# Reciprocals and accumulator adds on GpSimd, P^T written over P, and a new order: two concatenated attention blocks on one core

## The chip, the core and the metric

One core of a Trainium2 chip runs the whole program. The metric is the time of one execution on the device in microseconds (us); the median of the runs shown stands for a kernel. The engines are named as the profile names them: PE (TensorE), PEld (its weight loads), DVE (VectorE), ACT (ScalarE), POOL (GpSimd) and SP (SyncE, which here only issues transfers).

## The reference

Two attention blocks with one set of shapes, A with 4 key/value heads for 32 query heads and B with 32 of each. Their results are concatenated along the last axis.

```python
# B=16 sequences, Sq=32 query tokens, D=1024, 32 query heads, Sk=1024 keys, Dh=128; all bf16
def block(x, k_cache, v_cache, wq, wo):          # A: 4 kv heads, each repeated 8 times; B: 32 kv heads
    q = (x @ wq) split into 32 heads
    scores = einsum("bhqd,bhkd->bhqk", q, k) * Dh ** -0.5
    p = softmax(scores, axis=-1)
    o = einsum("bhqk,bhkd->bhqd", p, v)
    return merge_heads(o) @ wo
out = concatenate([block(A...), block(B...)], axis=-1)
```

## The kernel before

**Work units.** The attention is cut into quads of 128 rows: 128 of block A (four query heads that share one K and V) and 128 of block B (two heads of two sequences, four different K and V). One quad goes through a fixed line of steps: scores on PE into two PSUM banks (L1003 for A, L1032 for B, where two quads are made together from 32x32 pieces of the array); the negated row maximum on DVE (L1044); exp on ACT, which writes P in bf16 and the row sum into `stat` (L1057); four PE transposes of P, taken as pairs of bf16 in f32 (L1069); the copy of P^T out of PSUM (`PT_ev`, through the helper `evac`, L643); P^T times V (L1089 for A, L1102 for B); the reciprocal of the row sum on DVE (`st_recip`, L1110); the multiplication by it (`norm`, L1118 on ACT, L1119 on DVE); a PE transpose of the result (L1125) and its copy into `OTA_sb` or `OTB_sb`.

**Around the quads.** K of block B is transposed in place by DVE in 32x32 pieces (L984), K of block A by PE (L977). Query projections (L734, L753) feed later quads. When a group of quads is done, the output projection `oproj` (L823) makes 512-wide results in one PSUM bank each: the first block of heads of an output is copied into `acc` (f32, SBUF), 64 later results are added to it by DVE (L835), and the last ones are added with a bf16 result (L844, and L839 for the last row group), which is sent out: by POOL's queue (L847, seven times) and at the very end by SP's (L841).

**What sets the order.** `list_schedule` builds the whole program as a list before it is emitted. It knows a duration for each step (`DUR`), the transfers' times, the buffers of each kind (`SLOTS`: 8 PSUM banks, 4 buffers for P, 4 for P^T, 8 for `stat`, 6 for O), and where PE must read another 16 KB piece of its program (`FETCH_BLOCK`, `FETCH_US`, `pe_pos`). It picks the next instruction by ranks; `TUNE` names one of 16 rank rules for each stretch of 40 choices. Copies and `norm` may go to ACT or DVE (`evac` with no engine). Each engine then executes its own list in order and waits on semaphores for what others make; a transfer is issued by SP once the buffer that it overwrites has been read.

**Late in the program** buffers that are done with are used again: K of B also goes to `wq_sb`, V of B to `xT_sb`, `QT_sb` and at last to `KB_sb`, and P of some quads to `xT_sb`.

Of the kernel before, what the change touches and what calls it, by code (L numbers as in the profile page):

```python
# [34 lines left out]
            "qprojA": 4, "qprojB": 4, "oprojA": 4, "oprojB": 4, "xT_tr": 16}  # L35
FETCH_BLOCK = 252
FETCH_US = 6.2
LOOK = 0.35
# [3 lines left out]
FREE_BANKS = 2  # L42
WINDOW = 40
RANKS = ((3.5, 122, 0.35, 0.0, 0.3), (3.0, 122, 0.35, 0.0, 0.3), (4.0, 122, 0.35, 0.0, 0.3), (3.5, 122, 0.15, 0.0, 0.3), (2.5, 122, 0.35, 0.0, 0.3), (5.0, 122, 0.35, 0.0, 0.3),
         (3.5, 122, 0.7, 0.0, 0.3), (3.5, 120, 0.35, 0.0, 0.3), (3.0, 124, 0.2, 0.0, 0.3), (3.5, 122, 0.15, 1.5, 0.3), (3.5, 122, 0.15, -1.5, 0.3), (3.5, 122, 0.15, 0.0, 0.0),
         (3.5, 122, 0.15, 0.0, 0.7), (3.5, 122, 0.15, 4.0, 0.3), (3.5, 122, 0.15, -4.0, 0.3), (3.5, 122, 0.25, 0.0, 0.3))
TUNE = (2, 5, 12, 2, 2, 2, 8, 9, 10, 10, 2, 0, 14, 11, 6, 10, 5, 14, 7, 0, 1, 9, 11, 15, 15, 8, 8, 15, 11, 3, 3, 8, 6, 3, 4, 14, 2, 5, 1, 10, 10, 14, 3, 2, 7,
        14, 14, 14, 14, 14, 14, 7, 12, 3, 11, 1, 9, 9, 9, 0, 7, 12, 4, 10, 9, 0, 10, 1, 14, 7, 0, 10, 10, 3, 10, 12, 8, 8, 14, 15, 12, 0, 7, 2, 15, 12, 4, 1,
        13, 7, 11, 13, 13, 10, 11, 7, 12, 8, 7, 14, 5, 15, 2, 9, 6, 12, 8, 1, 12, 12, 8, 13, 12, 14, 13, 11, 1, 12, 2, 9, 14, 12, 4, 14, 2, 14, 6)
HOLD_AHEAD = 1  # L50
# [15 lines left out]
    "o_fin@act": (0.47, 0.13),  # L66
    "KBt_tr": (1.15, 0.11), "max": (1.12, 0.11), "recip": (0.06, 0.11), "norm@dve": (0.265, 0.13), "PT_ev@dve": (0.58, 0.12),
    "OT_ev@dve": (0.13, 0.12), "KTA_ev@dve": (0.58, 0.12), "QBt_tr": (0.345, 0.10), "acc+": (0.58, 0.12), "accF": (0.59, 0.12),
    "qA_ev@dve": (0.58, 0.12), "qB_ev@dve": (0.58, 0.12), "xT_ev@dve": (0.60, 0.12), "o_fin@dve": (0.58, 0.12), "QR_ev@dve": (0.58, 0.12),
# [45 lines left out]

SLOTS = {"bank": 8, "P": 4, "PT": 4, "stat": 8, "O": 6}

# [11 lines left out]
class Prog:  # L129
# [120 lines left out]
    def list_schedule(self, lat=0.05, look=LOOK):  # L250
# [144 lines left out]

        pe_pos = [0]
        pe_have = {0: 0.0, 1: 0.0}
# [23 lines left out]
        while True:  # L421
            best = None
            bkey = None
            turn = len(order) // WINDOW
            turn = TUNE[turn] if turn < len(TUNE) else 0
# [128 lines left out]
def build(nc, pa, pb, out):  # L554
# [34 lines left out]
    with stack:  # L589
# [6 lines left out]
        ident = sb("ident", [P, P], BF)  # L596
        id32 = sb("id32", [P, P], F32)
        stat = sb("stat", [P, SLOTS["stat"], 4], F32)
        xT_sb = sb("xT_sb", [P, 2, DJ, NTOK], BF)
# [15 lines left out]
        P_sb = sb("P_sb", [P, SLOTS["P"], Sk], BF)  # L615
        PT_sb = sb("PT_sb", [P, SLOTS["PT"], NCH, P], BF)
        O_sb = sb("O_sb", [P, SLOTS["O"], Dh], BF)
# [12 lines left out]
        for idt, key in ((ident, "ident"), (id32, "id32")):  # L630
            pr.add("pool", lambda g, idt=idt: g.memset(idt[:], 0.0), writes=[key], name="c0")
            pr.add("pool", lambda g, idt=idt: g.affine_select(idt[:], idt[:], [[1, P]], ALU.not_equal, 1.0, base=0, channel_multiplier=-1),
                   writes=[key], name="c1")

        def evac(dst_ap, src_ap, reads, writes, name, eng=None, wtag=None, rtag=None, mul=None):
# [172 lines left out]
        def oproj(pi, blk, G):  # L808
# [7 lines left out]
            for oh in range(NOH):  # L816
# [15 lines left out]
                if blk == 0:  # L832
                    evac(a_ap, lambda v=v: bank(v)[:, 0:OUTW], reads=[], writes=[v, ("acc", pi, G, oh)], name="acc0")
                elif blk < nblk - 1:
                    pr.add("dve", lambda e, a_ap=a_ap, v=v: e.tensor_tensor(a_ap, a_ap, bank(v)[:, 0:OUTW], ALU.add),  # L835
                           reads=[], writes=[v, ("acc", pi, G, oh)], name="acc+")
                elif final:
                    o_ap = woA_sb[:, oh, 0:OUTW]
                    pr.add("dve", lambda e, a_ap=a_ap, o_ap=o_ap, v=v: e.tensor_tensor(o_ap, a_ap, bank(v)[:, 0:OUTW], ALU.add),  # L839
                           reads=[("acc", pi, G, oh)], writes=[v, ("woA", oh)], name="accF")  # L840
                    pr.add("sp", lambda e, o_ap=o_ap, oh=oh: e.dma_start(out_flat[G * P:(G + 1) * P, cols[pi] + oh * OUTW:cols[pi] + (oh + 1) * OUTW], o_ap),  # L841
                           reads=[("woA", oh)], dma_key=f"outf{oh}", name="outh_dma", dur=P * OUTW * 2)
                else:
                    pr.add("dve", lambda e, a_ap=a_ap, o_ap=o_ap, v=v: e.tensor_tensor(o_ap, a_ap, bank(v)[:, 0:OUTW], ALU.add),  # L844
                           reads=[], writes=[v] + [("acc", pi, G, x) for x in range(oh + 1)], name="accF")
# [70 lines left out]
        XK = 4 * LATE + 4 + NKB  # L916
        XV = 2 * LATE + 2 + 1

# [28 lines left out]
        def tile_v(t, x):  # L947
# [62 lines left out]

        def pt_of(v):
            return PT_sb[:, v.idx, :, :].rearrange("p c q -> p (c q)") if isinstance(v, Virt) else p_of(v)

        def st_scoresB(qs):
            n = qs[0].pn
            for q in qs:
                score_buf(q)
                q.vP, q.vPT = (("xT", 0, q.e), ("xT", 0, 2 + q.e)) if n >= XT_FREE and n % 2 else (Virt("P"), Virt("PT"))
                q.vO = Virt("O")
# [16 lines left out]
            kt = [(home_k(4 * q0.pn + x), ("T", 4 * q0.pn + x)) for x in range(4)]  # L1036
            halves = [("KV", r_[1]) for r_, _ in kt] if 2 * n == V_LAST - 4 else []
            for fp_ in range(4):
# [23 lines left out]
        def st_ptr(q):  # L1062
            vP, vPT, vb = q.vP, q.vPT, q.vbt

            def e_pt(e):
# [4 lines left out]
                return last  # L1070
            pr.add("pe", e_pt, reads=[vP, "id32", vPT], writes=[vb], name="PT_trA" if q.pi == 0 else "PT_trB")

        def st_pev(q, eng=None):
            vPT, vb = q.vPT, q.vbt
            evac(lambda: pt_of(vPT).bitcast(F32), lambda: bank(vb), reads=[], writes=[vb, vPT],
                 name="PT_ev", eng=eng)

        def ptc_of(vPT, c, lo, hi):
            return pt_of(vPT).rearrange("p (m r two) -> p m r two", m=NPK, two=2)[:, c // 2, lo:hi, c % 2]

        def st_pvA(q):
            vPT, vb = q.vPT, q.vbo
            gp = (q.s * NG + q.G) % 2
            kvs = q.kvslot

            def e_pv(e):
                last = None
                for c in range(NCH):
                    last = e.matmul(bank(vb)[:, 0:Dh], ptc_of(vPT, c, 0, P), VA_sb[:, kvs, c, :], start=(c == 0), stop=(c == NCH - 1))  # L1089
                return last  # L1090
            pr.add("pe", e_pv, reads=[vPT, ("VA", kvs)], writes=[vb], claims=[("OT", 0, gp, q.hh0 + a_) for a_ in range(4)], name="PVA",
                   rtag={("VA", kvs): q.kid})

        def st_pvB(q):
            vPT, vb = q.vPT, q.vbo
            gp = (q.m * NG + q.G) % 2

            def e_pv(e):
                last = None
                for c in range(NCH):  # L1100
                    for x in range(4):
                        last = e.matmul(bank(vb)[32 * x:32 * x + 32, 0:Dh], ptc_of(vPT, c, 32 * x, 32 * x + 32), tile_v(q.t, x)[:, c * Dh:(c + 1) * Dh],  # L1102
                                        start=(c == 0), stop=(c == NCH - 1), tile_position=(0, 32 * x))
                return last
            pr.add("pe", e_pv, reads=[vPT] + [res_v(q.t, x) for x in range(4)], writes=[vb], claims=[("OT", 1, gp, q.e + 2 * i) for i in range(2)],
                   name="PVB", tag="B%d" % q.t, rtag=dict((res_v(q.t, x), ("V", q.t, x)) for x in range(4)))

        def st_recip(q):
            vst = q.vst
            pr.add("dve", lambda e: e.reciprocal(stat[:, vst.idx, 2:3], stat[:, vst.idx, 1:2]), writes=[vst], name="recip")  # L1110

# [229 lines left out]
```

## Time and profile before

| | |
|---|---|
| median of 3 runs (lowest, highest) | 842.84 us (841.28, 844.58) |
| the profiled execution | 842.9 us, of which the span of its instructions 841.1 us |
| busy in the span | PE 747.0, DVE 718.6, ACT 609.9, POOL 5.0 us |
| TensorE clock granted, mean | 0.985 |
| moved by the 16 DMA engines | 341.68 MB, 406 GB/s over the span |

The busy times are sums over the span. A row of groups gives the line, engine, operation, output and input, count, then busy us and mean ns of one, then the idle time before them and what ended most of it. A row of stages gives the busy us of each engine, the granted clock, the DMA engines' busy share and the rate.

### The profile page before, as it was taken

The numbers are of one execution on the slowest core, as the hardware profiler recorded it, in microseconds if no ns is written. First come the engines' busy times: TensorE is split into PE (matmuls) and PEld (weight loads), VectorE is DVE, ScalarE is ACT, GpSimd is POOL, SyncE is SP. The second block draws the span as 40 slices with busy tenths as digits, with TensorE's granted clock in tenths as the row PEclk, the third lists the DMA queues.
The fourth block names the chain that finished last, engine by engine and source line by source line (L and its number), as shares of the span: only waits on it lengthen the run. The fifth ranks groups of instructions, "written<-read, shape, count | busy, mean of one in ns | idle before, by whom it ended". The sixth has DMA issues, their size and how long they took to land.

```text
span 841.1 us, 29570 instructions
## 1 busy us (share of the span) xinstructions
PE 747.0 (89%) x12864; PEld 475.3 (57%) x12864; DVE 718.6 (85%) x1016; ACT 609.9 (73%) x1361; POOL 5.0 (1%) x15
## 2 busy tenths in 40 slices
PE   5979899999989989999898999899988888878877
PEld 3456566666556556555565565555655546555654
DVE  0588888989889889898998898898989879989996
ACT  3378778878868667678778777677867758776773
POOL 0000000000000000000000000000000000000000
PEclk9999999999999999999999999999999999989999
DMA  9999999999999999999999999999999999999994
GB/s 340 420 415 419 412 410 418 416 416 415 419 413 416 416 419 411 413 393 417 419 404 416 418 414 421 418 397 418 417 417 406 415 416 420 416 384 403 417 416 198
DMA packets 56144, 341.68 MB, mean 406 GB/s; under 512 B 16144, under 2 KB 16400, under 8 KB 25040
## 3 DMA queue, kind: packets, MB, share of 16 engines
q1 hardware_dynamic: 55456, 337.97, 98.1%
q8 instruction: 101, 1.65, 0.8%
q0 software_dynamic: 560, 1.84, 0.5%
q14 instruction: 27, 0.22, 0.1%
HBM read 337.64 MB, written 2.10 MB: 404 GB/s over the span
## 4 chain that ended last, share of the span: by engine, by line
PE 50%; DVE 18%; ACT 14%; DMA 13%; issue 3%; SPq 2%; DVEq 0%; ACTq 0%
PE psum L1069 11%; ACT P_sb L1057 9%; DVE stat L1044 8%; DMA KB_sb<-in_B_k_cache_dram 8%; PE psum L823 8%; DVE KB_sb L984 7%; PE psum L1032 6%; PE psum L1102 6%; PE psum L734 5%; PE psum L1089 4%; PE psum L753 4%; PE psum L1003 3%; DMA VB_sb<-in_B_v_cache_dram 2%; PE psum L977 2%; PE psum L1125 1%
## 5 line engine op out<-in xcount | busy, mean ns | idle before, releaser
L1044 DVE TENSOR_REDUCE stat<-psum 128x1 f32<-128x1024 f32 x256 | 302.7, 1209 | 48.2 <-PE psum L1032 30.7
L1057 ACT ACTIVATE P_sb<-psum,stat 128x1024 bf16<-128x1024 f32 x246 | 274.9, 1119 | 60.6 <-DVE stat L1044 57.9
L984 DVE STREAM_TRANSPOSE KB_sb<-KB_sb 128x1024 f32<-128x1024 f32 x240 | 284.7, 1221 | 15.4 <-DMA KB_sb<-in_B_k_cache_dram 15.0
L1069 PE MATMUL psum<-id,P_sb 128*128 128x128 f32 x984 | 170.1, 303 | 19.3 <-ACT P_sb L1057 15.3
L1069 PEld LDWEIGHTS psum<-id,P_sb 128*128 128x128 f32 x984 | 139.8, 209 | 56.4 <-ACT P_sb L1057 40.4
L643 ACT COPY PT_sb<-psum 128x512 f32<-128x512 f32 x232 | 132.7, 598 | 26.5 <-PE psum L1069 23.9
L1118 ACT ACTIVATE O_sb<-psum,stat 128x128 bf16<-128x128 f32 x216 | 78.0, 376 | 47.5 <-PE psum L1089 20.3
L1003 PE MATMUL psum<-KTA_sb,QT_sb 128*128 128x512 bf16 x256 | 80.7, 384 | 7.1 <-ACT P_sb L1057 6.3
L1089 PE MATMUL psum<-VA_sb,PT_sb 128*128 128x128 bf16 x1024 | 79.2, 222 | 7.0 <-ACT QR L643 2.1
L1032 PE MATMUL psum<-KB_sb,QR 32*32 32x512 bf16 x3840 | 74.8, 396 | 11.7 <-issue 4.8
L1089 PEld LDWEIGHTS psum<-VA_sb,PT_sb 128*128 128x128 bf16 x1024 | 63.4, 99 | 29.0 <-issue 10.5
L1102 PE MATMUL psum<-VB_sb,PT_sb 128*32 128x128 bf16 x3584 | 70.2, 223 | 9.7 <-issue 2.7
L753 PE MATMUL psum<-wq_sb,xT_sb 128*128 128x512 bf16 x256 | 69.3, 385 | 2.2 <-DMA wq_sb<-in_B_wq_dram 1.6
L823 PE MATMUL psum<-woB_sb,OTB_sb 128*128 128x512 bf16 x256 | 67.5, 381 | 3.6 <-ACT OTB_sb L643 1.2
L1102 PEld LDWEIGHTS psum<-VB_sb,PT_sb 128*32 128x32 bf16 x3584 | 52.4, 98 | 30.0 <-issue 10.9
L1032 PEld LDWEIGHTS psum<-KB_sb,QR 32*32 32x32 bf16 x3840 | 43.7, 89 | 37.4 <-ACT P_sb L1057 9.4
L823 PE MATMUL psum<-woA_sb,OTA_sb 128*128 128x512 bf16 x256 | 60.5, 380 | 1.5 <-ACT OTA_sb L643 0.8
L1125 PE MATMUL psum<-ident,O_sb 128*128 128x128 bf16 x256 | 49.7, 225 | 6.8 <-ACT O_sb L1118 3.9
L734 PE MATMUL psum<-xT_sb,wq_sb 128*128 128x512 bf16 x192 | 50.1, 380 | 0.3 <-ACT QR L643 0.3
L1057 ACT ACTIVATION_READ_ACCUMULATOR P_sb<-psum,stat 128x1 f32 x246 | 49.9, 203 | 0.0
L835 DVE TENSOR_TENSOR acc<-acc,psum 128x512 f32<-128x512 f32 x64 | 41.1, 674 | 8.4 <-PE psum L823 8.4
L1125 PEld LDWEIGHTS psum<-ident,O_sb 128*128 128x128 bf16 x256 | 23.4, 98 | 36.2 <-ACT O_sb L1118 16.2
(63 smaller groups left out, 585.8 us busy)
## 6 DMA issues: line engine op xcount, KB each, us to landing
KB_sb<-in_B_k_cache_dram SPq DMA_DIRECT2D x240, 512.0 KB, 11.0
VB_sb<-in_B_v_cache_dram SPq DMA_DIRECT2D x468, 256.0 KB, 8.1
KA_sb<-in_A_k_cache_dram SPq DMA_DIRECT2D x64, 256.0 KB, 10.2
VA_sb<-in_A_v_cache_dram SPq DMA_DIRECT2D x64, 256.0 KB, 9.8
wq_sb<-in_B_wq_dram SPq DMA_DIRECT2D x16, 512.0 KB, 8.9
woB_sb<-in_B_wo_dram SPq DMA_DIRECT2D x32, 256.0 KB, 9.8
woA_sb<-in_A_wo_dram SPq DMA_DIRECT2D x32, 256.0 KB, 8.7
wq_sb<-in_B_k_cache_dram SPq DMA_DIRECT2D x16, 512.0 KB, 10.2
```

The costliest lines, as they stand in the source:

```text
L643: return e.copy(dst, src) if hasattr(e, "activation") else e.tensor_copy(dst, src)
L734: last = e.matmul(bank(v)[:, 0:tn], w_[:, j, hh * Dh:(hh + 1) * Dh], xT_sb[:, 0, j, t0:t0 + tn], start=(j == 0), stop=(j == DJ - 1))
L753: last = e.matmul(bank(v)[:, 0:CW], xT_sb[:, 1, j, G * P:(G + 1) * P], wq_sb[:, j, mh * CW:(mh + 1) * CW], start=(j == 0), stop=(j == DJ - 1))
L823: last = e.matmul(bank(v)[:, 0:OUTW], OT[:, gp, hh, :], wo_[:, hh, oh * OUTW:(oh + 1) * OUTW], start=(hh == 0), stop=(hh == nh - 1))
L984: pr.add("dve", lambda e: e.transpose(tile_k(x).bitcast(F32), tile_k(x).bitcast(F32)), writes=[home_k(x)], name="KBt_tr", rtag={home_k(x): ...
L1003: pr.add("pe", lambda e, u=u: e.matmul(bank(vS[u]), qt[:, q.b, q.hh0:q.hh0 + 4, :].rearrange("p a q -> p (a q)"), KTA_sb[:, sl, u * 512:(u ...
L1032: last = e.matmul(bank(q.vS[g2])[32 * x:32 * x + 32, :].rearrange("p (s j) -> p s j", s=16), lhsT, rhs, start=(fp == 0), stop=(fp == 3), t ...
L1044: pr.add("dve", lambda e: e.tensor_reduce(stat[:, vst.idx, 0:1], both(vS), AXIS.XY, ALU.max, negate=True), writes=vS + [vst], name="max")
L1057: return e.activation(dst, src, ACTF.Exp, bias=stat[:, vst.idx, 0:1], scale=1.0, accum_out=stat[:, vst.idx, 1:2])
L1069: last = e.transpose(bank(vb)[:, m * P:(m + 1) * P], p32[:, m:Sk // 2:NPK], id32[:])
L1089: last = e.matmul(bank(vb)[:, 0:Dh], ptc_of(vPT, c, 0, P), VA_sb[:, kvs, c, :], start=(c == 0), stop=(c == NCH - 1))
L1102: last = e.matmul(bank(vb)[32 * x:32 * x + 32, 0:Dh], ptc_of(vPT, c, 32 * x, 32 * x + 32), tile_v(q.t, x)[:, c * Dh:(c + 1) * Dh], start=( ...
```

## The change

1. The 256 reciprocals of the row sums go from DVE to POOL, as a power of -1 (`tensor_tensor` with `ALU.pow` and a column of -1, `minus1`).
2. The 64 adds into `acc` go from DVE to POOL, which adds two SBUF operands. For that the result of the projection is first copied from PSUM into one of two new buffers, `part_sb` (by ACT or DVE, as the order decides).
3. P^T is written over P in the same buffer. `PT_sb` (4 buffers) is gone, and P has 6 instead of 4. Late in the program (from pair 54) P of every pair lies in `xT_sb`, before it was every second pair.
4. The order is made anew: another `TUNE`, other costs for the moved steps, 253 instead of 252 PE instructions in a 16 KB piece of the program, the first piece boundary moved by 70 instructions, and 5.8 instead of 6.2 us for reading one.
5. The rules for which late buffer holds what (`kb_of`, `res_v`, `XV`, `tile_v`) are written more generally.

```diff
-FETCH_BLOCK = 252
-FETCH_US = 6.2
+FETCH_BLOCK = 253
+FETCH_FIRST = 70
+FETCH_US = 5.8
...
-TUNE = (2, 5, 12, 2, 2, 2, 8, 9, 10, 10, 2, 0, 14, 11, 6, 10, 5, 14, 7, 0, 1, 9, 11, 15, 15, 8, 8, 15, 11, 3, 3, 8, 6, 3, 4, 14, 2, 5, 1, 10, 10, 14, 3, 2, 7,
+TUNE = (6, 5, 8, 3, 10, 12, 9, 9, 3, 9, 13, 14, 7, 9, 0, 2, 0, 8, 4, 13, 12, 12, 14, 5, 13, 14, 9, 14, 11, 11, 4, 12, 12, 14, 14, 14, 14, 14, 9, 8, 9, 9, 13,
...
-    "KBt_tr": (1.15, 0.11), "max": (1.12, 0.11), "recip": (0.06, 0.11), "norm@dve": (0.265, 0.13), "PT_ev@dve": (0.58, 0.12),
+    "KBt_tr": (1.15, 0.11), "max": (1.12, 0.11), "recip": (0.25, 0.15), "part@act": (0.47, 0.13), "part@dve": (0.58, 0.12), "norm@dve": (0.265, 0.13), "PT_ev@dve": (0.58, 0.12),
...
-SLOTS = {"bank": 8, "P": 4, "PT": 4, "stat": 8, "O": 6}
+SLOTS = {"bank": 8, "P": 6, "stat": 8, "O": 6, "part": 2}
...
-        pe_pos = [0]
+        pe_pos = [FETCH_FIRST]
...
-        PT_sb = sb("PT_sb", [P, SLOTS["PT"], NCH, P], BF)
+        part_sb = sb("part_sb", [P, SLOTS["part"], OUTW], F32)
...
+        pr.add("pool", lambda g: g.memset(minus1[:], -1.0), writes=["minus1"], name="c0")
...
                 elif blk < nblk - 1:
-                    pr.add("dve", lambda e, a_ap=a_ap, v=v: e.tensor_tensor(a_ap, a_ap, bank(v)[:, 0:OUTW], ALU.add),
-                           reads=[], writes=[v, ("acc", pi, G, oh)], name="acc+")
+                    vp = Virt("part")
+                    evac(lambda vp=vp: part_sb[:, vp.idx, :], lambda v=v: bank(v)[:, 0:OUTW], reads=[], writes=[v, vp], name="part")
+                    pr.add("pool", lambda e, a_ap=a_ap, vp=vp: e.tensor_tensor(a_ap, a_ap, part_sb[:, vp.idx, :], ALU.add),
+                           reads=[], writes=[vp, ("acc", pi, G, oh)], name="acc+")
...
-        XV = 2 * LATE + 2 + 1
+        XV = 2 * LATE + NVB
...
-                q.vP, q.vPT = (("xT", 0, q.e), ("xT", 0, 2 + q.e)) if n >= XT_FREE and n % 2 else (Virt("P"), Virt("PT"))
+                q.vP = ("xT", 0, 2 * (n % 2) + q.e) if n >= XT_FREE else Virt("P")
...
-            evac(lambda: pt_of(vPT).bitcast(F32), lambda: bank(vb), reads=[], writes=[vb, vPT],
+            evac(lambda: p_of(vP).bitcast(F32), lambda: bank(vb), reads=[], writes=[vb, vP],
                  name="PT_ev", eng=eng)
...
-            pr.add("dve", lambda e: e.reciprocal(stat[:, vst.idx, 2:3], stat[:, vst.idx, 1:2]), writes=[vst], name="recip")
+            pr.add("pool", lambda e: e.tensor_tensor(stat[:, vst.idx, 2:3], stat[:, vst.idx, 1:2], minus1[:], ALU.pow), reads=["minus1"], writes=[vst], name="recip")
```

**The first place is where the adds into `acc` begin, about a fifth of the way in.** DVE before, where L1044 is the row maximum, L984 the transpose of K, L1110 the reciprocal and L835 the add:

```order
L1110 RECIPROCAL stat<-stat 128x1 x2
L1119 TENSOR_SCALAR O_sb<-psum,stat 128x128
L984 STREAM_TRANSPOSE KB_sb<-KB_sb 128x1024
L1044 TENSOR_REDUCE stat<-psum 128x1 x2
L984 STREAM_TRANSPOSE KB_sb<-KB_sb 128x1024 x3
L835 TENSOR_TENSOR acc<-acc,psum 128x512 x2
L1110 RECIPROCAL stat<-stat 128x1 x3
```

POOL after, from its last preparation to the fourth row of adds (L1115 is the reciprocal, L844 the add):

```order
L640 MEMSET minus 128x1
L1115 TENSOR_TENSOR stat<-stat,minus 128x1 x45
L844 TENSOR_TENSOR acc<-acc,part_sb 128x512 x2
L1115 TENSOR_TENSOR stat<-stat,minus 128x1 x4
L844 TENSOR_TENSOR acc<-acc,part_sb 128x512
L1115 TENSOR_TENSOR stat<-stat,minus 128x1 x2
L844 TENSOR_TENSOR acc<-acc,part_sb 128x512
L1115 TENSOR_TENSOR stat<-stat,minus 128x1 x11
L844 TENSOR_TENSOR acc<-acc,part_sb 128x512 x2
```

Reciprocals and adds have left DVE's list and share POOL's, so that a reciprocal stands behind stretches of one to four adds. Of the 64 copies that feed the adds the new order puts 56 on ACT and 8 on DVE.

**The second place is DVE's end**, from the transposes of the last K of block B (in `KB_sb`, then `wq_sb`) to the last row maximum. Before:

```order
L984 STREAM_TRANSPOSE KB_sb<-KB_sb 128x1024 x4
L984 STREAM_TRANSPOSE wq_sb<-wq_sb 128x1024 x3
L1044 TENSOR_REDUCE stat<-psum 128x1
L984 STREAM_TRANSPOSE wq_sb<-wq_sb 128x1024
L844 TENSOR_TENSOR acc<-acc,psum 128x512 x2
L1044 TENSOR_REDUCE stat<-psum 128x1
L1110 RECIPROCAL stat<-stat 128x1 x3
L1119 TENSOR_SCALAR O_sb<-psum,stat 128x128 x2
L1044 TENSOR_REDUCE stat<-psum 128x1 x2
```

And after, where the last adds are L853, the maximum L1049 and `norm` L1124:

```order
L992 STREAM_TRANSPOSE KB_sb<-KB_sb 128x1024 x4
L992 STREAM_TRANSPOSE wq_sb<-wq_sb 128x1024
L1049 TENSOR_REDUCE stat<-psum 128x1
L992 STREAM_TRANSPOSE wq_sb<-wq_sb 128x1024
L853 TENSOR_TENSOR acc<-acc,psum 128x512
L992 STREAM_TRANSPOSE wq_sb<-wq_sb 128x1024
L853 TENSOR_TENSOR acc<-acc,psum 128x512
L992 STREAM_TRANSPOSE wq_sb<-wq_sb 128x1024
L1049 TENSOR_REDUCE stat<-psum 128x1 x3
L1124 TENSOR_SCALAR O_sb<-psum,stat 128x128 x2
```

The adds moved ahead of the last transposes, the two `norm` behind the last maximum, and the reciprocals away.

**The third place is PE's end**, from the P^T of the last quads to the last projection. Before (L1102 is P^T times V, L823 the projection, L1125 the transpose of its input):

```order
L1069 MATMUL psum<-id,xT_sb 128x128 x4
L1125 MATMUL psum<-ident,O_sb 128x128 x2
L823 MATMUL psum<-woB_sb,OTB_sb 128x512 x2
L1102 MATMUL psum<-KB_sb,xT_sb 32x128 x32
L823 MATMUL psum<-woB_sb,OTB_sb 128x512 x2
L1125 MATMUL psum<-ident,O_sb 128x128
L823 MATMUL psum<-woB_sb,OTB_sb 128x512 x2
L1102 MATMUL psum<-KB_sb,xT_sb 32x128 x32
L823 MATMUL psum<-woB_sb,OTB_sb 128x512 x2
L1125 MATMUL psum<-ident,O_sb 128x128
L823 MATMUL psum<-woB_sb,OTB_sb 128x512 x4
```

And after (L1107, L830, L1130):

```order
L1074 MATMUL psum<-id,xT_sb 128x128 x12
L1107 MATMUL psum<-xT_sb 32x128 x32
L1107 MATMUL psum<-KB_sb,xT_sb 32x128 x32
L1130 MATMUL psum<-ident,O_sb 128x128 x2
L830 MATMUL psum<-woB_sb,OTB_sb 128x512 x2
L1107 MATMUL psum<-KB_sb,xT_sb 32x128 x32
L830 MATMUL psum<-woB_sb,OTB_sb 128x512 x4
L1130 MATMUL psum<-ident,O_sb 128x128
L830 MATMUL psum<-woB_sb,OTB_sb 128x512 x6
```

The P^T transposes of three quads now stand together, and after the last product with V ten projection matmuls are left where there were six.

49 lines of the change are left out of this document (25 added, 24 removed).

## The prediction

> **What bounds the kernel now.** I read the page first: its busy times and its slices.
>
> ```profile
> PE 747.0 (89%) x12864; PEld 475.3 (57%) x12864; DVE 718.6 (85%) x1016; ACT 609.9 (73%) x1361; POOL 5.0 (1%) x15
> ...
> DMA  9999999999999999999999999999999999999994
> GB/s 340 420 415 419 412 410 418 416 416 415 419 413 416 416 419 411 413 393 417 419 404 416 418 414 421 418 397 418 417 417 406 415 416 420 416 384 403 417 416 198
> ```
>
> PE and DVE look like the bound, but the transfers fill the span: the DMA engines are busy by nine tenths or more in 39 of 40 slices, at 410 to 421 GB/s in most. Then the view by stages, in windows of 20 us, with three short ones at the end (columns: us, PE, PEld, DVE, ACT, POOL busy, granted clock, DMA share, GB/s).
>
> ```profile
> 20.00:40.00 20.00, 20.00 (x167) 10.18 (x165) 9.78 (x11) 8.02 (x13) 0.00 (x0) 0.98 1.01 421
> 360.00:380.00 20.00, 19.86 (x313) 12.20 (x311) 18.93 (x31) 15.37 (x36) 0.00 (x0) 1.00 1.00 389
> 740.00:760.00 20.00, 17.11 (x286) 11.85 (x285) 15.58 (x24) 12.45 (x33) 0.00 (x0) 0.83 0.96 380
> 828.00:830.00 2.00, 1.74 (x39) 1.27 (x40) 2.00 (x2) 1.52 (x5) 0.00 (x0) 1.00 0.43 170
> ```
>
> A full queue reads 1.00 or 1.01 (transfers overlap a little). At 360:380 the rate is low with the engines still full, so that is a slower kind of transfer and no wait. Of the 20 us windows between 20 and 820 us only 740:760 falls below 1.00. The stream of inputs ends at 829 us, and about 12 us of arithmetic follow. So the time is a stream of 829 us that nothing can shorten but its dips, and a tail. PE, DVE and ACT matter where they let the stream run dry, and in the tail.
>
> **The change part by part, against 842.9 us (span 841.1 and 1.8 around it; the median shown is 842.84, so both can be compared with the result as they stand).** Durations come from the groups by line and form:
>
> ```profile
> L1044 DVE TENSOR_REDUCE stat<-psum 128x1 f32<-128x1024 f32 x256 | 302.7, 1209 | 48.2 <-PE psum L1032 30.7 <-PE psum L1003 15.8 <-PE psum L777 0.7
> L984 DVE STREAM_TRANSPOSE KB_sb<-KB_sb 128x1024 f32<-128x1024 f32 x240 | 284.7, 1221 | 15.4 <-DMA KB_sb<-in_B_k_cache_dram 15.0
> L643 ACT COPY PT_sb<-psum 128x512 f32<-128x512 f32 x232 | 132.7, 598 | 26.5 <-PE psum L1069 23.9
> L835 DVE TENSOR_TENSOR acc<-acc,psum 128x512 f32<-128x512 f32 x64 | 41.1, 674 | 8.4 <-PE psum L823 8.4
> L1110 DVE RECIPROCAL stat<-stat 128x1 f32<-128x1 f32 x256 | 29.6, 145 | 7.7 <-ACT P_sb L1057 6.5
> L632 POOL TENSOR_SCALAR_AFFINE_SELECT id<-id 128x128 f32<-128x128 f32 x1 | 0.3, 282 | 0.1
> L1326 POOL MEMSET const-float32-1.0<- 128x1 f32 x1 | 0.1, 98 | 0.0
> ```
>
> *DVE* loses 29.6 + 41.1 = 70.7 us. Eight of the new copies land on it, at 674 ns by the add of the same shape: 8 x 0.674 = 5.4. So 718.6 - 70.7 + 5.4 = 653 us, 78% of the span. *ACT* gets 56 copies of 0.598 = 33.5 us, so 643 us. Neither is the bound, so in the stream this is worth nothing by itself: the transfers cover it.
>
> *POOL* gets 256 powers and 64 adds, and no row shows either. A power on one column lies between POOL's cheapest row, 0.10 (98 ns), and its dearest computing row, 0.28; I take 0.28, as that one computes. An add: from 98 ns for 1 element to 282 for 128 is 1.45 ns an element, so 512 elements cost 0.098 + 512 x 1.45 ns = 0.84 us with one operand, and 0.098 + 512 x 2.9 ns = 1.58 us if a second operand costs as much again; I take 1.2, the middle. Together 256 x 0.28 + 64 x 1.2 = 149 us (from 26 + 54 = 80 to 72 + 101 = 173), at most a fifth of the span. [...]
>
> What does a reciprocal on POOL delay? Only `norm` needs it. From the end of an exp to `norm` stand P^T on PE, its copy and the product with V. Their rows, in the last quads (timeline):
>
> ```profile
> 831.74 0.75 PE L1069 MATMUL psum<-id,xT_sb 128*128 128x128 f32 x4
> 832.68 0.59 ACT L643 COPY xT_sb<-psum 128x512 f32<-128x512 f32 x1
> 832.96 0.63 PE L1102 MATMUL psum<-KB_sb,xT_sb 128*32 128x128 bf16 x32
> 835.13 0.63 PE L1102 MATMUL psum<-KB_sb,xT_sb 128*32 128x128 bf16 x32
> ```
>
> That is 0.75 + 0.59 + 0.63 = 1.97 us of cover at the least. A power alone (0.28), or behind one add (1.48), is hidden; behind two adds (0.28 + 2.4 = 2.68) it is up to 0.7 us late. And today the reciprocal is late too, by DVE's queue, which the waits show:
>
> ```profile
> ACT O_sb L1118 <- DVE stat L1110: 10.2, 13, 1.9
> SPq L649 <- PE psum L1003: 3.9, 2, 3.3
> KB_sb<-in_B_k_cache_dram SPq DMA_DIRECT2D x240, 512.0 KB, 11.0
> ```
>
> (The second row is SP's queue within 735 to 762 us, the third the issues.) 13 waits with 10.2 us go, some like them come back behind pairs of adds: nothing, with the transfers as cover. If that cover is gone, a late `norm` holds a PSUM bank, PE stands, and SP can't issue. How far the cover reaches: 512 KB land 11.0 us after issue, though at 418 GB/s they need 1.3, so most of the rest is queue. The one dip of the stream stands beside a wait of SP of 3.3 us.
>
> *P^T over P.* The copy already waits for the transposes that read P, so the new hazard adds no wait. A buffer is now held from exp to the product with V, so six take the place of four and four. Nothing, from 1 us either way.
>
> *The order in the stream.* The dip at 740:760 costs (1.01 - 0.96) x 20 = 1.0 us; I count it as gone. If every slice under 418 GB/s between the first and the last rose to it, the sum of the shortfalls (185 GB/s x 21.03 us / 418) would be 9.3 us, but most of those slices have full queues; I bound the gain at 3 us. Downwards, new dips: up to 3 us, three like this one.
>
> *The tail* I read from the chain that ended last, and from the timeline behind it:
>
> ```profile
> 810.36 1.32 issue
> 814.53 4.53 DVE KB_sb L984 x4
> 819.06 3.38 DVE wq_sb L984 x3
> 822.44 1.11 DVE stat L1044
> 823.55 1.15 DVE wq_sb L984
> 824.70 0.58 DVE acc L844
> 825.37 0.69 DVE acc L844
> 826.06 1.14 DVE stat L1044
> ...
> 827.11 0.27 DVE L1110 RECIPROCAL stat<-stat 128x1 f32<-128x1 f32 x3
> 827.36 0.61 DVE L1119 TENSOR_SCALAR O_sb<-psum,stat 128x128 bf16<-128x128 f32 x2
> 827.89 2.35 DVE L1044 TENSOR_REDUCE stat<-psum 128x1 f32<-128x1024 f32 x2
> ...
> 830.27 1.11 ACT L1057 ACTIVATE xT_sb<-psum,stat 128x1024 bf16<-128x1024 f32 x1
> 837.42 1.29 DVE L839 TENSOR_TENSOR woA_sb<-acc,psum 128x512 bf16<-128x512 f32 x2 [2.57 <-PE psum L823]
> ```
>
> The tail hangs on DVE: from 814.53 to 830.24 it works without a pause towards the last maximum. The new order keeps there eight transposes, one maximum, two adds and three maxima, and puts the two `norm` behind them and the reciprocals away: -0.27 - 0.61, of which a maximum's start takes back a little; -0.7. Ahead of it PE stood 1.32 us for its program ("issue" on the chain); the new order knows the places of these reads better, but some read falls into the tail all the same: half, -0.6 (0 to -1.3). Behind the last exp (ends 831.4) I follow PE's new list: two P^T of 0.75, products of the quads before, then the last product, then four matmuls ahead of the last transpose and six after it instead of two and four. Two steps of two matmuls are 2 x 0.54 by the chain row
>
> ```profile
> 833.59 0.54 PE psum L823 x2
> ```
>
> so +1.1, while the 2.17 us between the last two products (832.96, 835.13) shrink a little: +0.9 net (from -1 to +1.5). Tail: -0.7 - 0.6 + 0.9 = -0.4 (from -3 to +1.5).
>
> Sum: 842.9 - 1.0 (stream) - 0.4 (tail) = **841.5 us**.
>
> **Rivals.** *More is won (836.5 to 839).* The new order's map of PE's program reads is exact, dips go (-3) and the tail starts earlier (-3): 842.9 - 6 = 836.9. For it: 101 pieces of program over the span, and waits of PE for "issue" of up to 2.6 us, one of them in the dip's stretch. Against: those waits did not empty the queue anywhere else.
>
> ```profile
> PEld psum L1102 <- issue: 12.9, 25, 2.6
> q8 instruction: 101, 1.65, 0.8%
> ```
>
> [...]
>
> *Slower: POOL's list holds up PE.* An add waits for its copy, the copy for a projection; every reciprocal behind it waits as well. Where that comes to more than 1.97 us behind an exp, `norm` is late, a bank stays taken, PE stands, SP stands. The price is a dip of 1.0 us each time the delay outlasts the queue. POOL's list has 34 stretches of one to four adds; if a third of them cost one dip, 11 us: 842.9 + 11 - 1 = 853. It decides from about five such dips (4.2 us). For it: a queue with two jobs, and the order rests on durations that POOL may not keep. Against: 13 late reciprocals today did not empty the stream. If a power cost 2.9 us or more, POOL would itself be the bound (256 x 2.9 + 77 = 819), ten times its nearest row.
>
> **How the numbers follow.** 0.5% of the time, 4.2 us, is about what a measurement of this kernel can tell from no change: faster means below 838.6, slower above 847.1. Forecast (stream full, tail about as before, 839 to 844): 0.48. More is won: 0.24, of which 0.22 below 838.6, as the floor of 836.9 and the line lie close. Lock or new small dips (842 to 847), nothing gained: 0.12. POOL's list: 0.16, above 847. The range takes from 836.5, the floor, to 847.5, where the slower rival begins.
>
> **What would show it.** Right: DMA shares of 1.00 and more in all windows to 820 us; the end of the stream within 2 us of 829; DVE near 653, ACT near 643, POOL between 80 and 173 us; transposes on DVE still near 1220 ns; `norm` waiting for POOL less than 20 us in all. Wrong: windows under 0.96 beside stretches of adds, a power above 1 us, transposes that grow while POOL adds, a tail of more than 14 us behind the stream.

## The result and the profile after

| | before | after |
|---|---|---|
| median, us (lowest to highest, runs) | 843.28 (841.28 to 844.58, 4) | 888.45 (888.2 to 890.28, 4) |
| the profiled execution / its span, us | 842.9 / 841.1 | 888.53 / 886.8 |
| TensorE clock granted, mean | 0.985 | 0.975 |

The ratio after to before is 1.0541, with a 95% interval of 1.0517 to 1.0566: 5.4% slower, 45 us, where 841.5 us had been forecast and 847.5 was the upper end. Of the runs reported below, one of experiment 1 (855.05 us) and one of experiment 10 (856.34 us) lay more than 1.5% above the fastest run of their kernel and are left out of medians and ratios.

The first lines to read are the same as before, the page's busy times and the last rows of its slices.

```profile
PE 744.2 (84%) x12731; PEld 473.7 (53%) x12864; DVE 678.9 (77%) x701; ACT 635.1 (72%) x1420; POOL 225.4 (25%) x336
...
DMA  9999999999999999999999999999999999999995
GB/s 330 394 394 388 397 396 394 392 392 389 393 396 359 394 390 396 395 389 396 395 394 392 394 390 395 393 385 388 398 393 385 393 394 392 395 396 383 398 394 190
```

No engine is near the span, and the DMA engines are as full as before. What changed is what a full queue moves: 388 to 398 GB/s in most slices, where it was 410 to 421. The stages say the same, more sharply (columns as in the prediction: us, PE, PEld, DVE, ACT, POOL busy, granted clock, DMA share, GB/s):

```profile
20.00:40.00 20.00, 19.74 (x162) 9.87 (x165) 10.38 (x11) 9.39 (x17) 1.66 (x3) 1.00 1.03 399
260.00:280.00 20.00, 16.68 (x277) 11.53 (x249) 12.17 (x14) 11.00 (x29) 2.74 (x5) 0.77 0.95 356
360.00:380.00 20.00, 15.70 (x235) 9.23 (x236) 17.69 (x17) 16.21 (x36) 6.34 (x9) 1.00 1.00 391
740.00:760.00 20.00, 17.09 (x313) 11.17 (x318) 17.47 (x19) 15.22 (x36) 5.79 (x8) 1.00 1.01 395
876.00:878.00 2.00, 2.00 (x40) 1.88 (x42) 0.26 (x1) 1.16 (x3) 0.08 (x1) 0.83 0.33 125
```

In 20:40 the rate is 399 GB/s at a share of 1.03; before it was 421 at 1.01. POOL works 1.66 of these 20 us, in three instructions, so its work is hardly what slows the queue. The ratio of these two rates is 1.055, that of the times 1.054. The stream now ends at about 878 us (the last input landed at 878.7, before at 830.3, by the trace's packets: 48.4 us later), and the tail behind it is shorter than it was, 8.1 instead of 10.9 us. So the whole loss lies in the stream, nearly evenly, from its first microseconds on, and its share of busy time does not show it. One window, 260:280, also falls short in its share (0.95), which is worth (1.01 - 0.95) x 20 = 1.2 us; it is taken up with experiments 11 and 12.

Behind slower transfers the engines wait longer. The waits of after (engine, buffer, line, what is waited for: us in all, times, longest), and then its issues (last figure: median us from issue to landing):

```profile
DVE KB_sb L992 <- DMA KB_sb<-in_B_k_cache_dram: 46.9, 41, 3.2
PEld psum L1107 <- DMA VB_sb<-in_B_v_cache_dram: 28.0, 24, 2.7
ACT O_sb L1123 <- POOL stat L1115: 0.2, 1, 0.2
```

```profile
KB_sb<-in_B_k_cache_dram SPq DMA_DIRECT2D x240, 512.0 KB, 12.7
VB_sb<-in_B_v_cache_dram SPq DMA_DIRECT2D x468, 256.0 KB, 10.2
```

DVE's wait for K was 15.0 us and is 46.9; 512 KB of K landed 11.0 us after their issue and now land after 12.7. `norm` hardly waits for POOL's reciprocals at all: once, 0.2 us.

What the moved work itself costs stands in the groups:

```profile
L1049 DVE TENSOR_REDUCE stat<-psum 128x1 f32<-128x1024 f32 x256 | 300.9, 1209 | 101.4 <-PE psum L1037 63.1 <-PE psum L1011 31.4 <-PE psum L784 6.5
L992 DVE STREAM_TRANSPOSE KB_sb<-KB_sb 128x1024 f32<-128x1024 f32 x240 | 287.4, 1226 | 49.2 <-DMA KB_sb<-in_B_k_cache_dram 46.9
L1115 POOL TENSOR_TENSOR stat<-stat,minus 128x1 f32<-128x1 f32 x256 | 140.3, 548 | 580.2 <-ACT P_sb L1062 539.3 <-ACT xT_sb L1062 40.7
L844 POOL TENSOR_TENSOR acc<-acc,part_sb 128x512 f32<-128x512 f32 x64 | 80.5, 1275 | 55.1 <-ACT part_sb L650 45.5 <-DVE part_sb L650 9.6
```

A power takes 548 ns, an add 1275, and DVE's transposes beside them 1226 ns where they took 1221.

**Single packets.** The trace holds every packet of the DMA engines with its size and duration. Grouped by size, they give the mean in ns (the 16 KB packets without those of the program):

| packet | what it fills | number | before | after |
|---|---|---|---|---|
| 8 KB | four partition rows of 2 KB (V of B above all) | 22817 | 318.1 | 339.9 |
| 16 KB | four rows of 4 KB (K of B) | 8192 | 621.4 | 646.7 |
| 2 KB | one row | 8192 | 86.5 | 89.1 |

Every kind takes longer, by 2.6 to 6.3 ns for each row written. 22817 x 21.8 + 8192 x 25.3 + 8192 x 2.6 ns = 726 us, over 16 engines 45 us: the loss.

**What can make a packet longer?** The kernel issues the same transfers from the same inputs. But the buffers that they fill lie elsewhere. In the built program, buffers are laid out one behind another in a partition, in steps of 32 bytes. The change also adds the 4-byte column of -1, `minus1`, and allocates it ahead of `stat` and of every buffer that a transfer fills (the diff ahead of the prediction doesn't show that line). Before, `xT_sb` starts at byte 17408 = 68 x 256 of a partition, and every buffer that a transfer fills starts at a multiple of 1024, and so of 256. After, `xT_sb` starts at 17440, and each of them is 32 bytes off.

### The profile page after: what moved, and what is told of

Its sections match the earlier page's. It is cut to its first block, busy times and chain, and to the rows that moved or that the text cites. A ratio compares the mean times of both kernels' runs of the same rounds, so it can differ in the third digit from the quotient of the medians.

```text
span 886.8 us, 29585 instructions
## 1 busy us (share of the span) xinstructions
PE 744.2 (84%) x12731; PEld 473.7 (53%) x12864; DVE 678.9 (77%) x701; ACT 635.1 (72%) x1420; POOL 225.4 (25%) x336
## 4 chain that ended last, share of the span: by engine, by line
DMA 41%; PE 28%; DVE 12%; ACT 9%; SPq 6%; issue 3%; DVEq 0%; ACTq 0%
DMA KB_sb<-in_B_k_cache_dram 15%; DMA VB_sb<-in_B_v_cache_dram 13%; SPq L656 5%; DVE stat L1049 5%; PE psum L1074 5%; ACT P_sb L1062 5%; PE psum L830 4%; PE psum L1037 4%; DMA VA_sb<-in_A_v_cache_dram 4%; DVE KB_sb L992 4%; DMA KA_sb<-in_A_k_cache_dram 4%; PE psum L1107 3%; PE psum L741 3%; PE psum L1094 2%; PE psum L760 2%
## 5 line engine op out<-in xcount | busy, mean ns | idle before, releaser
L1049 DVE TENSOR_REDUCE stat<-psum 128x1 f32<-128x1024 f32 x256 | 300.9, 1209 | 101.4 <-PE psum L1037 63.1
L992 DVE STREAM_TRANSPOSE KB_sb<-KB_sb 128x1024 f32<-128x1024 f32 x240 | 287.4, 1226 | 49.2 <-DMA KB_sb<-in_B_k_cache_dram 46.9
L1062 ACT ACTIVATE P_sb<-psum,stat 128x1024 bf16<-128x1024 f32 x236 | 263.0, 1117 | 62.3 <-DVE stat L1049 61.3
L1115 POOL TENSOR_TENSOR stat<-stat,minus 128x1 f32<-128x1 f32 x256 | 140.3, 548 | 580.2 <-ACT P_sb L1062 539.3
L1074 PE MATMUL psum<-id,P_sb 128*128 128x128 f32 x944 | 161.8, 301 | 26.1 <-ACT P_sb L1062 21.9
L650 ACT COPY P_sb<-psum 128x512 f32<-128x512 f32 x216 | 123.9, 595 | 29.2 <-PE psum L1074 27.3
L844 POOL TENSOR_TENSOR acc<-acc,part_sb 128x512 f32<-128x512 f32 x64 | 80.5, 1275 | 55.1 <-ACT part_sb L650 45.5
L1094 PE MATMUL psum<-VA_sb,P_sb 128*128 128x128 bf16 x1024 | 79.0, 223 | 11.6 <-DMA VA_sb<-in_A_v_cache_dram 3.9
L1107 PE MATMUL psum<-VB_sb,P_sb 128*32 128x128 bf16 x3392 | 66.8, 222 | 25.5 <-DMA VB_sb<-in_B_v_cache_dram 20.9
L1094 PEld LDWEIGHTS psum<-VA_sb,P_sb 128*128 128x128 bf16 x1024 | 62.6, 99 | 33.8 <-issue 12.6
L1011 PE MATMUL psum<-KTA_sb,QT_sb 128*128 128x512 bf16 x214 | 69.8, 385 | 7.2 <-issue 1.8
L1107 PEld LDWEIGHTS psum<-VB_sb,P_sb 128*32 128x32 bf16 x3392 | 49.2, 97 | 49.5 <-DMA VB_sb<-in_B_v_cache_dram 28.0
L830 PE MATMUL psum<-woB_sb,OTB_sb 128*128 128x512 bf16 x235 | 66.1, 398 | 9.9 <-ACT P_sb L1062 2.3
L830 PE MATMUL psum<-woA_sb,OTA_sb 128*128 128x512 bf16 x235 | 56.5, 379 | 5.4 <-issue 1.7
L1130 PE MATMUL psum<-ident,O_sb 128*128 128x128 bf16 x256 | 52.1, 228 | 9.3 <-ACT O_sb L1123 6.5
L741 PE MATMUL psum<-xT_sb,wq_sb 128*128 128x512 bf16 x170 | 46.9, 384 | 3.3 <-issue 1.5
## 6 DMA issues: line engine op xcount, KB each, us to landing
KB_sb<-in_B_k_cache_dram SPq DMA_DIRECT2D x240, 512.0 KB, 12.7
```

Source lines behind the costliest of these rows:

```text
L650: return e.copy(dst, src) if hasattr(e, "activation") else e.tensor_copy(dst, src)
L830: last = e.matmul(bank(v)[:, 0:OUTW], OT[:, gp, hh, :], wo_[:, hh, oh * OUTW:(oh + 1) * OUTW], start=(hh == 0), stop=(hh == nh - 1))
L992: pr.add("dve", lambda e: e.transpose(tile_k(x).bitcast(F32), tile_k(x).bitcast(F32)), writes=[home_k(x)], name="KBt_tr", rtag={home_k(x): ...
L1049: pr.add("dve", lambda e: e.tensor_reduce(stat[:, vst.idx, 0:1], both(vS), AXIS.XY, ALU.max, negate=True), writes=vS + [vst], name="max")
L1062: return e.activation(dst, src, ACTF.Exp, bias=stat[:, vst.idx, 0:1], scale=1.0, accum_out=stat[:, vst.idx, 1:2])
L1074: last = e.transpose(bank(vb)[:, m * P:(m + 1) * P], p32[:, m:Sk // 2:NPK], id32[:])
```

## The experiments

Two theories were set against each other first. *Addresses*: the 32 bytes of the new column make every packet longer, and the rest of the change is worth about nothing. *The work itself*: POOL's reading and writing of SBUF, the new order, or P^T over P slows the transfers. The kernel before was run again beside each set of experiments, hence its several medians, from 842.8 to 843.55 us.

**1. The column behind all buffers** (after, one line moved):

```diff
-        minus1 = sb("minus1", [P, 1], F32)
         stat = sb("stat", [P, SLOTS["stat"], 4], F32)
...
         O_sb = sb("O_sb", [P, SLOTS["O"], Dh], BF)
+        minus1 = sb("minus1", [P, 1], F32)
```

> The changed kernel, with the column of -1 placed behind all other buffers instead of ahead of them; every buffer that a transfer writes then starts at the address that it had in the kernel before (a multiple of 512 bytes, as the kernel before has it, not 32 bytes past one). Nothing else changes. Address theory (the 32 bytes slow every transfer): the stream is back at 413 to 421 GB/s, 8 KB packets at about 318 ns instead of 340, time 837 to 846 us. GpSimd theory (its powers and adds slow the transfers or the engines): stream stays near 394 GB/s, time 884 to 890. Order theory (the new lists cost it): as the GpSimd theory, 884 to 890.

Measured: 846.14 us (11 runs, 840.55 to 849.79), before 843.55 (17 runs); ratio 1.0024 (1.0002 to 1.0045). That is just above the 846 at which the address theory's range ended. 8 KB packets are back at 317.8 ns. The page's rate:

```profile
GB/s 332 417 419 398 419 421 418 415 415 410 393 405 327 420 408 416 419 412 418 419 418 415 419 414 418 418 409 405 416 418 413 410 418 418 419 419 403 417 381 167
```

All of the work of the change is still there, the full slices are back at 415 to 421 GB/s, and 42 of the 45 us are gone. A hole in the 13th slice is left (327), which after has too (359); it is taken up with experiments 11 and 12.

**2. to 6. The other way round: before, with nothing but a pad** behind `id32`, of 32, 64, 128, 256 and 512 bytes in turn:

```diff
         id32 = sb("id32", [P, P], F32)
+        pad = sb("pad", [P, 1], F32)    # 4 bytes, takes 32; then 16, 32, 64, 128 columns
         stat = sb("stat", [P, SLOTS["stat"], 4], F32)
```

> The kernel before with one unused column of 4 bytes ahead of stat, which moves all later buffers up by 32 bytes, and nothing else: same lists, no work on GpSimd. Address theory: stream near 394 GB/s, 8 KB packets near 340 ns, time 884 to 892 us. GpSimd theory and order theory: no change, 841 to 845.

> The kernel before with 64 unused bytes at the same place, all later buffers 64 bytes further. Address theory with a step of 64 bytes (what counts is a start at a multiple of 64): 841 to 846 us. Address theory with a coarser step (128, 256 or 512): slower, 860 to 892. The other two theories: 841 to 846.

> The kernel before with 128 unused bytes at the same place. Address theory with a step of 64 or 128 bytes: 841 to 846 us. With a step of 256 or 512: 860 to 892. The other two theories: 841 to 846.

> The kernel before with 256 unused bytes ahead of stat, all later buffers 256 bytes further. Address theory, step of 256 bytes: 841 to 846 us, stream at 413 to 421 GB/s. Step of 512 bytes or more: 878 to 888, stream near 396 GB/s, as 32, 64 and 128 bytes gave.

> The kernel before with 512 unused bytes at the same place. Address theory, step of 256 or 512 bytes: 841 to 846 us. Step of 1024 bytes (the buffers of the kernel before start at multiples of 1024): 878 to 888.

| pad, bytes | us (runs) | 8 KB packet, ns |
|---|---|---|
| none | 843.55 (17); beside the last two rows 842.8 (13) | 318.1 |
| 32 | 887.52 (4); ratio 1.0524 (1.0501 to 1.0548) | 340.8 |
| 64 | 885.47 (1) | 339.4 |
| 128 | 882.93 (1) | 338.6 |
| 256 | 842.71 (1) | 317.8 |
| 512 | 843.07 (1) | 318.0 |

The rates of the kernels with 32 and with 256 bytes, in this order:

```profile
GB/s 329 395 393 392 392 395 395 390 397 391 396 390 391 393 394 394 393 368 398 395 392 377 384 393 394 397 382 392 396 394 391 395 396 394 395 387 392 396 399 212
```

```profile
GB/s 333 418 420 415 416 415 419 415 415 417 417 415 414 417 418 414 406 394 419 419 410 416 421 413 420 419 405 414 404 417 407 406 421 416 419 385 398 419 417 210
```

The kernel before, with not one instruction changed, becomes as slow as the kernel after when its buffers move by 32 bytes, and is itself again when they move by 256. So the place of the buffers is sufficient for the loss (experiment 2) and necessary for all but about 3 of its 45 us (experiment 1). The price does not grow with the shift: one of 128 bytes costs no more than one of 32 (338.6 ns a packet against 340.8). In packets of four rows it is 5.5 ns for a row of 2 KB and 6.3 ns for a row of 4 KB (before to after), so it goes with the rows rather than with their bytes. Shifts of 32, 64 and 128 bytes have it, those of 256 and 512 do not, which of the steps that were tried fits 256 alone. What in a shifted row takes the time was not shown.

**7. Only V of B off its place** (32 bytes ahead of `VB_sb`, 480 behind it, so that what follows is back at a multiple of 512):

```diff
+        pad = sb("pad", [P, 8], F32)
         VB_sb = sb("VB_sb", [P, NVB, 4, NCH * Dh], BF)
+        pad2 = sb("pad2", [P, 120], F32)
```

> The kernel before with 32 unused bytes ahead of VB_sb and 480 behind it: of the buffers that transfers write, VB_sb alone starts 32 bytes past a multiple of 512. Its 468 transfers of 256 KB are 14976 of the 22817 packets of 8 KB. Address theory, a cost per packet that falls only on the packets to a shifted buffer: 14976 x 22 ns over 16 engines = 20.6 us, 862 to 866. If one shifted buffer slows the whole stream: 878 to 888. If the shift matters in another buffer (not in VB_sb): 841 to 846.

Measured: 857.84 us (1 run; before 842.8). The 16 KB packets stay as they were (623.6 ns), the mean 8 KB packet takes 328.8. The rate is between the two:

```profile
GB/s 336 409 412 406 407 409 407 405 409 408 410 404 403 408 410 390 403 407 410 409 397 390 410 407 410 406 406 410 405 410 383 399 412 410 411 410 412 413 397 203
```

The bill by packets closes again: (328.8 - 318.1) x 22817 / 16 = 15.3 us, and the time rose by 15.0. The expectation was 20.6 us, from 22 ns for each of the 14976 packets that fill `VB_sb` (468 transfers of 32 packets); the mean comes to 16 ns for each of them. So the loss goes with the shifted buffer, as K's packets lose nothing, but it is smaller than expected. The trace narrows this down. Of the 8 KB packets 10985 still took under 320 ns, at least 3144 more than the 7841 (22817 - 14976) that go to other buffers; in experiment 2 only 1396 did. Those that took 320 to 400 ns had a mean of 335.7 ns, in experiment 2 of 337.9. So a slowed packet cost about the same in both, but with the neighbours in place at least a fifth of the shifted buffer's packets were not slowed. Why was not settled.

**8. Each power computed twice** (experiment 1, with a first power into an unused column of `stat`), to see what POOL's work is worth:

```diff
+            def emit(e):
+                e.tensor_tensor(stat[:, vst.idx, 3:4], stat[:, vst.idx, 1:2], minus1[:], ALU.pow)
+                return e.tensor_tensor(stat[:, vst.idx, 2:3], stat[:, vst.idx, 1:2], minus1[:], ALU.pow)
```

> The changed kernel with the column of -1 placed last, and every reciprocal computed twice on GpSimd (the first result into an unused column of stat), which adds 256 x 0.55 = 141 us of work there. If GpSimd's list holds PE up (the rival of late reciprocals), the time grows over 846 us by 4 us or more, with norm waiting for GpSimd well over 10 us in all; if the cover of exp to norm hides it, 842 to 849, as with one power.

Measured: 845.9 us (10 runs), before 842.8 (13 runs); ratio 1.0049 (1.0027 to 1.0071), against 1.0024 (1.0002 to 1.0045) for experiment 1: the intervals overlap. The page:

```profile
PE 735.7 (87%) x12731; PEld 471.2 (56%) x12864; DVE 674.6 (80%) x701; ACT 633.9 (75%) x1420; POOL 357.7 (42%) x592
```

POOL works 132 us more, and the time is within the scatter of experiment 1 (846.14). No wait of `norm` for POOL is among the waits. So nothing of the power's 548 ns shows on the path.

**9. Before's lists, with the reciprocals as powers on POOL**, and **10. after's lists, with the reciprocals on DVE** (both with the column last):

```diff
@@ 9: before's list is built with the reciprocal on DVE, and the instruction put on POOL when it is rebuilt
+            if name == "recip":
+                eng, reads = "pool", reads + ("id32",)
@@ 10: experiment 1, the other way round
+            if name == "recip":
+                eng = "dve"
```

> The kernel before with its lists kept in order, except that the 256 reciprocals go to GpSimd as powers, each in its old place among the others; the column of -1 is placed last, so the buffers keep their addresses. What is left over of the change at the old addresses (1.0024) may come from GpSimd's powers or from the new lists. If the powers cost it (0.55 us each instead of 0.15, ahead of norm): 845 to 848 us. If the new lists cost it: 841 to 844, and less if DVE, 30 us lighter, frees buffers earlier; the stream's bytes keep it above 838.

> The changed kernel with the column of -1 placed last and its lists kept in order, except that the 256 reciprocals stay on DVE, each in its place among the others. If the powers on GpSimd cost what is left over (1.0024): 842 to 844 us. If the new lists cost it, and a lighter DVE does not matter: 845 to 848, as with the powers. If DVE's 30 us matter: above 848.

Measured: experiment 9 842.98 us (11 runs), ratio 0.9999 (0.9988 to 1.0009); experiment 10 846.5 us (11 runs), ratio 1.0032 (1.0021 to 1.0043); before 843.12 (23 runs). Busy times, 9 and then 10:

```profile
PE 736.1 (87%) x12734; PEld 478.6 (57%) x12864; DVE 701.1 (83%) x760; ACT 609.2 (72%) x1361; POOL 144.1 (17%) x272
```

```profile
PE 735.2 (87%) x12731; PEld 473.2 (56%) x12864; DVE 691.6 (82%) x957; ACT 634.6 (75%) x1420; POOL 85.7 (10%) x80
```

256 reciprocals moved to POOL are worth nothing that these runs resolve: within 0.1% with the old order, and with the new one the intervals of experiments 1 and 10 overlap. What is left of the change at the old addresses, 0.2 to 0.3% (0.5% in experiment 8), comes with the new lists (the order, P^T over P and the adds on POOL, which were not tried apart).

**11. and 12. The hole in the 13th slice.** The profiles of experiments 1, 8 and 10, with the new lists and the old addresses, all have it (327, 326 and 356 GB/s). In experiment 1 it lies at 260 to 270 us:

```profile
255.00:260.00 5.00, 4.59 (x28) 2.87 (x28) 3.92 (x4) 2.88 (x6) 0.56 (x2) 0.66 1.02 413
260.00:265.00 5.00, 5.00 (x100) 4.07 (x102) 4.19 (x4) 4.19 (x12) 0.54 (x1) 1.00 0.56 213
265.00:270.00 5.00, 5.00 (x110) 3.14 (x98) 3.57 (x6) 3.32 (x9) 1.10 (x2) 1.00 0.87 269
```

The waits in 245 to 275 us, and of SP's queue in 250 to 275, name "issue", a wait for nothing that the profile shows, and, on SP, scores of PE that free a buffer:

```profile
PEld psum L1037 <- issue: 3.3, 1, 3.3
PE psum L1037 <- issue: 3.0, 1, 3.0
SPq L656 <- PE psum L1011: 3.9, 1, 3.9
```

On the chain that ended last PE stands from 252.4 to 255.4 us, and a 16 KB packet of its program's queue starts at 253.1 us, within that wait. If a read of the program at this place is the cause, moving all reads against the work must take the hole away. Experiment 1 got 32, then 64 transposes of the identity ahead of PE's first instruction, while PE waits for data:

```diff
+                if eng_name == "pe" and op is first_pe:
...
+                    for _ in range(32):        # 12: 64
+                        self.extra(eng)        # e.transpose(bankx(), ident[:], ident[:])
```

> The changed kernel with the column of -1 behind all buffers, and 32 transposes of the identity into a PSUM bank that is written over later, ahead of PE's first instruction (64 PE instructions with their weight loads, about 2 to 3 us in the first 3.7 us, in which PE waits for data). Every read of PE's program falls 64 instructions earlier in the work; no list is changed. Theory 'place of a program read': the dip of the transfers at 255 to 270 us (327, 326 and 356 GB/s in slice 13 of the three kernels with these lists) comes from a read of PE's program that falls on a step the transfers wait for. It then goes from slice 13 (above 400 GB/s), and may come back smaller elsewhere; the time is 843 to 846. Rival 'the order itself': the dip stays in slice 13 at 320 to 360 GB/s, the time 846 to 847.

> The same with 64 transposes (128 PE instructions, about 4 to 5 us, of which up to 2 lie behind PE's first wait for data). Place of a program read: slice 13 above 400 GB/s here too, time 843 to 847, as half a piece moves every read to another place, for better or worse. The order itself: slice 13 at 320 to 360 GB/s as before. If slice 13 is back in one of the two kernels only, the dip needs both the place and the order.

Measured: 843.87 us (10 runs), ratio 1.0021 (1.0001 to 1.0041), and 845.81 us (10 runs), ratio 1.0033 (1.0013 to 1.0053); before 843.03 (19 runs). The rates, 11 and then 12, and the stage of the hole in 11:

```profile
GB/s 333 419 417 379 419 419 418 415 418 403 417 418 416 418 418 418 403 387 406 399 411 407 419 412 419 420 418 415 418 419 405 408 416 418 418 420 417 420 410 138
```

```profile
GB/s 329 420 417 385 421 419 417 416 419 407 416 420 415 420 418 407 415 407 419 419 415 409 420 414 401 404 415 415 395 412 389 403 422 415 416 417 419 421 416 246
```

```profile
260.00:265.00 5.00, 4.87 (x41) 3.17 (x42) 4.32 (x5) 4.42 (x8) 1.19 (x3) 1.00 1.04 428
```

The hole is gone in both (416 and 415 GB/s), with the lists untouched, and so is the wait ahead of it: from 245 to 285 us no wait of PE for "issue" is longer than 0.6 us, where experiments 1, 8 and 10 have one of 3.3, 2.1 and 1.8. That speaks for the place of a program read, and against the order by itself. One rival stays open: the granted clock ahead of the hole was 0.66 in experiment 1 (255:260; 0.50 in experiment 8 and 0.79 in 10), and 1.00 in 11 and 12. Elsewhere in experiment 1 a low clock emptied nothing (0.83 in 720:740, at a share of 1.01), but the wait and the clock were not tried apart. And each kernel has one profile only, of a run of 849.8 us in experiment 1 and of 847.2 and 841.9 in 11 and 12.

The time did not follow. The intervals overlap that of experiment 1 (in 12 the 64 transposes also put off PE's first real work, from 3.7 to 7.8 us): smaller holes stand elsewhere (379 and 385 in the 4th slice, which was 398 in experiment 1; 387 in the 18th of 11, 389 in the 31st of 12), and the runs scatter as widely as those of experiment 1 (842.1 to 848.3, 841.9 to 849.0). So no single hole explains the last 0.2 to 0.3%, and its cause stays open. No version measured beats the kernel before.

## Why the prediction was wrong

*The step that failed* is its first conclusion: "the time is a stream of 829 us that nothing can shorten but its dips". The stream was taken as a fixed length, and the change was searched only for what could leave the queue empty. It forgot the other factor: how long a packet takes. That depends on where the packet goes too (8 KB took 318.1 ns in before, 339.9 into buffers 32 bytes further on), and the change moved all its targets. The new column was costed at nothing without a word, as 4 bytes that no transfer touches; its place was worth 42 us in experiment 1 and 44 in experiment 2. Nothing in the trace of before showed this price, as there every buffer that a transfer fills lay at a multiple of 256. But it could have been asked: the lists of instructions and the durations of operations say nothing about addresses, and the allocation is a list like any other.

*The tests it set itself* could only half see this. DMA shares of 1.00 and more in all windows: three windows of after fell short (0.95 in 260:280, 0.99 in 580:600 and in 800:820), worth 1.2 + 0.4 + 0.4 = 2 us at most. In all others the share was full, and no comfort: it read 1.03 in 20:40 with the longer packets (339.9 ns on the mean) and 1.01 with the shorter ones (318.1). The end of the stream within 2 us of 829: wrong by some 50 us (the last input landed at 878.7), and this was the test that caught it. POOL's busy time lay above its range. The column of GB/s at a full share, which the prediction read to find dips, was the one to compare. It even held a case: 389 GB/s at a share of 1.00 in 360:380 was put down to "a slower kind of transfer", and what makes one slower was not asked.

*None of its rivals* was this. "POOL's list holds up PE" had the sign, but not the mechanism: `norm` waited 0.2 us for POOL in after and 0.9 in experiment 1, and twice the powers changed nothing.

*Steps that held.* Transposes on DVE near 1220 ns: 1226 in after, beside 225.4 us of work on POOL, and 1220 in experiment 1, against 1221 before; so no run shows the lock that its chances name. Reciprocals on POOL worth nothing in the stream: shown by experiments 8, 9 and 10; that the cover of 1.97 us is the reason fits the rare waits of `norm` for POOL. POOL far from being the bound. The dip at 740:760: gone (share 1.01 in after), as counted, but another came at 260:280 (0.95 in after, 0.86 in experiment 1), so the 1.0 us was not won.

*Terms that were mis-sized.*

| term | predicted | measured |
|---|---|---|
| power on POOL, us each | 0.28 (0.10 to 0.28) | 0.55 |
| add on POOL, us each | 1.2 (0.84 to 1.58) | 1.28 |
| POOL in all, us | 149 (80 to 173) | 225.4 |
| DVE in all, us | 653 | 678.9 |
| ACT in all, us | 643 | 635.1 |
| tail, change in us | -0.4 (-3 to +1.5) | -2.8 (after), +1.2 (experiment 1) |

The tail alone settles little: with the same lists it was 7.4 us in the profile of experiment 12 and 12.9 in that of 11, against 10.9 before. The power's upper end was POOL's dearest row of another operation, which bounds nothing. For DVE, the groups' times were subtracted from the page's busy time. But the groups overlap, and busy time counts an overlap once: before, DVE's groups add up to 757.8 us against 718.6 busy. Experiment 9 shows it alone: without 29.6 us of reciprocals DVE's busy time fell by only 17.5. The new list also gave DVE more copies of other kinds than it had (20 of P^T instead of 14, 17 of K of A instead of 9).

*Program reads.* The prediction put the new map of the reads at -0.6 us in the tail, and a rival at -3 more in the stream. Experiments 11 and 12 speak for it that the place of a read can make or remove a hole (327 GB/s in the 13th slice of experiment 1, 416 and 415 in them). But the new map did not reduce the waits: those of PE's weight loads for "issue", among which a wait for the program would stand, came to 52.8 us in 115 waits before and 59.5 in experiment 9, with the old lists, and to 77.8 us in 175 waits in experiment 1 and 68.5 to 80.2 in experiments 8 and 10 to 12, with the new ones (sums of the rows).

With the place of the column put right, the kernel measures 846.14 us, inside the forecast's range of 836.5 to 847.5, and on the other side of its centre: the small gains that the forecast counted did not come.

## What to carry to other kernels

In this kernel, which is bound by its transfers, the start address of the buffers that a DMA fills was a part of its speed: 32 bytes past a multiple of 256 cost 5.2% (experiment 2), 256 bytes further on nothing (842.71 us against 842.8, experiment 5). In a kernel like it, put small columns behind the large buffers, or pad them, and look at every start modulo 256 bytes when an allocation is added. When the DMA share is full, compare GB/s at equal share, early in the program where nothing else differs; here the rate was low from early on (399 against 421 GB/s in 20:40, at shares of 1.03 and 1.01), and that pointed at the packets, not at waits. And when a change does several things, the line that does no work still has to be costed.

## What the runs showed of the hardware that was not expected

A transfer into SBUF rows that start 32, 64 or 128 bytes past a multiple of 256 took 339 to 341 ns for a packet of four 2 KB rows instead of 318, and 645 to 647 instead of 621 for four 4 KB rows; with shifts of 256 and 512 the packet of 2 KB rows took 317.8 and 318.0. For the kernel the first three were 4.7 to 5.2%, at a full DMA share (1.02 to 1.03 in 20:40, before 1.01). With one buffer shifted among others in place, its packets cost only 16 ns more on the mean, instead of 22, as at least a fifth of them were not slowed.

A power on one column of 128 rows took GpSimd 548 ns, beside 138 to 145 ns for DVE's reciprocal of the same column (experiment 10 and before); an add of two 128x512 f32 operands in SBUF took it 1275 ns, beside 674 ns for DVE's add with one operand in PSUM.
